# Two more units of a recurrent-attention kernel loaded as 32x32 blocks and turned by VectorE

## The chip, the cores and the metric

The kernel runs on one core of a Trainium2 chip. The metric is the device time of one execution in microseconds. The core has five engines with queues of their own: TensorE (PE; its weight loads are shown apart as PEld), VectorE (DVE), ScalarE (ACT), GpSimd (POOL) and SyncE (SP), which here issues nearly all DMAs.

## What is computed

An attention of the linear, gated kind (float32, B = 4 batches, H = 8 heads, S = 768 steps, D = 48 features) is followed by a feed-forward layer with a maximum over three products:

```python
f = 1.0 / (1.0 + np.exp(-f_logit))
for t in range(S):
    state = f[:, :, t, :, None] * state + np.einsum('bhd,bhe->bhde', k[:, :, t], v[:, :, t])
    y[:, :, t] = np.einsum('bhd,bhde->bhe', q[:, :, t], state)
x = y.transpose(0, 2, 1, 3).reshape(B * S, H * D)          # 3072 x 384
h = np.maximum(np.maximum(x @ w1, x @ w2), x @ w3)         # 384 -> 768
out = h @ w_out                                            # 768 -> 384
```

The weights come as 64-bit floats; the kernel turns them into 32-bit ones itself.

## The kernel before

**Units.** The attention is cut into 24 units (`NU`). A unit is a chunk of 64 time steps (`C`) of two batches with all eight heads: 128 rows of tokens. Even and odd units take the two pairs of batches. Four units make a group (`GRP`); the feed-forward layer works on groups of 512 tokens.

**One unit.** The gate f, the keys k and the queries q are needed with features on the partitions and time along the free dimension. The sigmoid of f (`sigmoids`) gives the gate; a scan along time from behind (`scan`, L329) gives factors r for the keys, and one from the front (`before`, L347) gives `prod` for the queries. `kh` = k turned times r (`after`, L340), `qh` = q turned times `prod` (L351). `pairs` multiplies kh and qh on TensorE (L392) and VectorE applies the causal mask (`at`, L395). `values` multiplies that with v (L411, L407 in the first group), `sums` adds the unit's keys times values to the state (L436 on TensorE, L444 on VectorE), for which the keys are needed once more with tokens on the partitions (`ks`). `finish` (L500) adds the share of the old state and ScalarE copies the result into `xT` (L506).

**Two ways to turn.** Units below `BY_ROWS` are loaded by rows: one DMA of 192 KB for each of f, k and q (L174), with tokens on the partitions and features along the free dimension. TensorE then turns them with four transposes each (`transposed`, L291) into PSUM. ScalarE takes the sigmoid from PSUM into the gate (L308), and VectorE multiplies kh and qh from PSUM. `keys` turns kh back with four TensorE transposes (L367), and ScalarE copies them into `ks` (L369).

Units from `BY_ROWS` on are loaded in pairs as blocks: eight DMAs of 64 or 32 KB for each of f, k and q (L183), which put every 32x32 block of tokens by features at the partitions where its features will lie. ScalarE takes the sigmoid from SBUF (L311), VectorE turns gate, kt and qt with one instruction each (`turned`, L296), and GpSimd multiplies kh and qh. `keys_by_blocks` makes `ks` with 16 instructions of VectorE (L382), four at each of four places of the loop.

Both ways share the same buffers: `room` holds four slots of a unit for each of f, k and q, in two tiles. Unit u by rows uses slot u % 4; a pair by blocks uses tile u // 2 % 2 as a whole.

**The weights.** 24 pieces are loaded into `raw` and `placed` and rounded to float32: ScalarE prepares (L240, L241, L244), VectorE joins the high bits (L254), and GpSimd adds the rest (L258) into `w_in` or, for pieces 18 to 23, into `w_out`. `apart` (L715) subtracts the first weight matrix from the other two. So the maximum becomes a linear part plus a maximum against zero.

**The first group.** `ffn_first` runs along with units 4 to 8. It computes the products of x with the weights (L537, two of the PSUM banks of pool `ps_f`), takes ScalarE's copy (L765) and VectorE's maximum (L767) into `hm`, turns the first weight matrix (`turn`, L737 and L738), forms the linear part's matrix (`linear`, L745, copied by L749), places the weights for the later groups by DMA (`place`, L454 and L461), and computes the outputs (`outputs`, L563). GpSimd's `mix_in` (L805) and `mix` (L587) prepare sums of weights. The later groups run with fewer products, from `placed` and mixed weights (L836, L609).

**Order.** The order is written out by hand, and the instructions of each engine stand in that order. In the loop over units 4 to 23, `fill(part)` puts a budgeted share of the feed-forward work between the steps of the attention. Each engine works through its own queue in order; semaphores tie them together. Which PSUM bank of a pool a new tile gets is settled when the program is built.

Of the kernel before, what the change touches and what calls it, by code (L numbers as in the profile page):

```python
# [55 lines left out]
def kernel(  # L56
# [15 lines left out]
    NU = B // 2 * (S // C)  # L72
# [5 lines left out]
    GRP = 4  # L78
# [11 lines left out]
    def fast():  # L90
        ctx = ExitStack()
        with ctx:
# [55 lines left out]
                    nc.vector.memset(t.rearrange("p (h d) -> p h d", d=DP)[:, :, D:], 0.0)  # L148

            NLD = 4  # L150
            BY_ROWS = 8
            v_tiles = [keep.tile([128, H, DP], FP32, name=f"v_ld{i}") for i in range(NLD)]
            for t in v_tiles:
                nc.gpsimd.memset(t[:, :, D:DP], 0.0)
# [12 lines left out]
            def load(u, queues=one, names="fkq"):  # L167
                for nm, src in (("f", f_logit), ("k", k), ("q", q)):
                    if nm not in names:
                        continue  # L170
                    if u < BY_ROWS:

# [114 lines left out]
            def transposed(nm, u, name="tr"):  # L287

                t = {"tr": ps_tr, "p": ps_f}[name].tile([128, HP, 2, C], FP32, name=name)
                for hp in range(HP):  # L290
                    nc.tensor.transpose(t[:, hp].rearrange("p a t -> p t a"), slots[nm][u % 4][:, hp * 128:(hp + 1) * 128],  # L291
                                        ident)
                return t.rearrange("p h a t -> p a h t")

            def turned(out, x):
                nc.vector.transpose(out.rearrange("p x (n t) -> p x n t", t=32), x.rearrange("p n x d -> p x n d"))  # L296
# [8 lines left out]
            def sigmoids(u):  # L305
                gate = gate_tiles[u % 2]
                if u < BY_ROWS:
                    nc.scalar.activation(by_batch(gate)[:, :, :, 1:], transposed("f", u), AF.Sigmoid)  # L308
# [5 lines left out]
            def features(nm, u):  # L314

                if u < BY_ROWS:
                    return transposed(nm, u, "p" if u < GRP - 1 else "tr")
# [6 lines left out]
            def scan(u):  # L324
                gate = gate_tiles[u % 2]
                if u >= BY_ROWS:
                    turned(gate[:, :, 1:], ready[u])
# [6 lines left out]
            def after(u):  # L334
# [4 lines left out]
                nc.gpsimd.tensor_copy(ends[:, u, :], whole)  # L339
                (nc.vector if u < BY_ROWS else nc.gpsimd).tensor_tensor(  # L340
                    kh.rearrange("p h a t -> p a h t"), kt,
# [3 lines left out]
            def before(u):  # L345
# [4 lines left out]
                qh = by_batch(work.tile([128, 2 * HP, C], FP32, name="qh", bufs=3))  # L350
                (nc.vector if u < BY_ROWS else nc.gpsimd).tensor_tensor(qh, qt, by_batch(prod[:, :, 1:]), op=ALU.mult)  # L351
                ready[u]["qh"] = qh
# [8 lines left out]
            def keys(u):  # L361

                if u < min(BY_ROWS, NU - 2):
                    kh = ready[u]["kh"]
                    tr_s = ps_tr.tile([UT, HP, 128], FP32, name="tr")
                    for hp in range(HP):
                        nc.tensor.transpose(tr_s[:, hp, :], kh[:, hp].rearrange("p a t -> p (a t)"), ident)  # L367
                    ks = work.tile([UT, H, DP], FP32, name="ks")
                    nc.scalar.copy(ks.rearrange("s h d -> s (h d)"), tr_s.rearrange("s a d -> s (a d)"))  # L369
                    ready[u]["ks"] = ks  # L370

            def keys_by_blocks(u, n):

                if BY_ROWS <= u < NU - 2:
                    kh = ready[u]["kh"]
                    if n == 0:
                        ready[u]["ks"] = work.tile([UT, H, DP], FP32, name="ks")
                    ks = ready[u]["ks"].rearrange("s (hp par) d -> s hp par d", par=2)
                    a, t0 = divmod(n * 32, C)
                    for p0 in range(0, 128, 32):  # L380
                        par, e0 = divmod(p0, DP)
                        nc.vector.transpose(ks[n * 32:(n + 1) * 32, :, par, e0:e0 + 32], kh[p0:p0 + 32, :, a, t0:t0 + 32])  # L382
# [131 lines left out]
            def pack(u0, u1, xT, queues=one):  # L514

                t = slice(u0 * UT, (u1 + 1) * UT)
                for par in range(2):
                    p0 = par * DP
                    queues[par].dma_start(out=xT[p0 + D:p0 + DP, 0:NK, t], in_=xT[p0:p0 + D, NK, t])
# [399 lines left out]
            def fill(ns):  # L919
                budget[0] += ns  # L920
                while budget[0] > 0 and pending:
                    try:
                        budget[0] -= next(pending[0])
                    except StopIteration:
                        pending.pop(0)
# [18 lines left out]
            with tc.manual_schedule():  # L944
# [78 lines left out]
                for u in range(GRP, NU):  # L1023
                    n = u + 1
                    part = EARLY if u < 2 * GRP else PART
                    fill(part)
                    keys(u)
                    keys_by_blocks(u, 2)
                    if u > GRP:
                        finish(u - 1, xT)  # L1030
                        if u % GRP == 3:
                            pack(0, 2, xT)
                        elif u % GRP == 0:
                            pack(3, 3, xT)
                    if u % GRP == 0:
                        if u > GRP:
                            packed[u // GRP - 1] = xT
                            pending.append(ffn(u // GRP - 1, xT))
                        xT = x_tiles[u // GRP % 2]
                    pairs(u)  # L1040

                    if u + 2 < BY_ROWS:
                        load(u + 2)
                    if BY_ROWS <= u + 3 < NU and u % 2:
                        load(u + 3, one, "fkq" if u % GRP == 1 else "f")
                    if u + 2 < NU:
                        load_v(u + 2)
                    if n < NU:
                        if n < BY_ROWS:
                            sigmoids(n)  # L1050
                        scan(n)
                    check_range(u - CHECKS, 0)
                    fill(part)
                    keys_by_blocks(u, 3)
                    if n < NU:
                        after(n)
                        before(n)
                    fill(part)
                    if BY_ROWS <= u + 2 < NU and u % GRP == 0:
                        load(u + 2, one, "k")  # L1060
                    values(u)
                    if n < NU:
                        carry(n)
                    check_range(u - CHECKS, 1)
                    fill(part)
                    if BY_ROWS <= u + 2 < NU and u % GRP == 0:
                        load(u + 2, one, "q")
                    keys_by_blocks(n, 0)
                    fill(part - 1000 if u < 2 * GRP else part)
                    keys_by_blocks(n, 1)  # L1070
                    check_range(u - CHECKS, 2)
                    if u + 2 >= CHECKS:
                        check_load(u + 2 - CHECKS)
                    if BY_ROWS <= u + 2 < NU:
                        sigmoids(u + 2)
# [272 lines left out]
```

## Time and profile before

| quantity | before |
|---|---|
| median of 3 runs (lowest to highest) | 423.31 us (423.26 to 423.86) |
| profiled execution: its time, and its span | 423.43 us, 421.7 us |
| busy TensorE, VectorE, ScalarE, GpSimd | 402.8, 264.5, 180.2, 235.2 us |
| mean granted clock of TensorE | 0.996 |
| turns of f, k, q on TensorE (L291): matrix instructions, length of one | 96, 0.27 us |
| turns of keys on TensorE (L367) | 32, 0.27 us |
| turns on VectorE: gate, kt, qt (L296) | 48, 0.66 to 0.72 us |
| turns of keys on VectorE (L382) | 224, 0.30 us |
| mean DMA share from 50 to 63.4, 63.4 to 78.3, 78.3 to 95, 95 to 106 us | 0.93, 0.72, 0.82, 0.25 |

Times in profile rows are microseconds from the span's start unless marked ns. A row of a timeline has start, length, engine, line, operation, output and inputs with their shapes, and a count; in brackets stand the idle time of the engine ahead of it and what ended it. Matrix instructions overlap, so a step of TensorE is best measured from one row's start to the next one's. The profiled execution's time is longer than its span by what lies around it. TensorE transposes one 128x128 float32 tile in an instruction, and a row "x4" is one of f, k, q or the keys of one unit.

### The profile page before, as it was taken

What the parts mean: (1) busy time and instruction counts of PE and PEld (TensorE: products, weight loads), DVE (VectorE), ACT (ScalarE), POOL (GpSimd) and SP (SyncE); (2) the same over time, 40 slices, a digit from 0 to 9 for tenths busy, and PEclk for the clock granted to TensorE, in tenths of its full rate; (3) what the DMA queues carried; (4) which work ended last, traced back from release to release, by engine and by line L of the source; (5) the groups of instructions that cost most, each with busy time, mean ns of one, the idle gap of its engine ahead of it and who ended that gap; (6) DMA issues with size and microseconds to landing.
All of it is one profiled execution on the core that took longest, in us unless ns stands there. A gap on an engine that the chain in (4) does not pass through costs nothing.

```text
span 421.7 us, 11556 instructions
## 1 busy us (share of the span) xinstructions
PE 402.8 (96%) x4650; PEld 338.5 (80%) x4650; DVE 264.5 (63%) x515; ACT 180.2 (43%) x414; POOL 235.2 (56%) x262
## 2 busy tenths in 40 slices
PE   4978899899999999999999999999999999999995
PEld 3756765466668888998889988889988889988994
DVE  6986594843597699868789867889764730002300
ACT  2478676632114442425531444442254524576210
POOL 2189554621988676376586357576556960435600
PEclk9999999999999999999999999999999999999998
DMA  8999897782547654277645276635473010542002
GB/s 169 232 266 284 236 258 112 121 170 67 102 85 129 87 116 66 60 106 101 117 104 95 56 113 87 144 79 89 64 144 91 11 54 9 158 140 75 2 19 60
DMA packets 175129, 47.20 MB, mean 112 GB/s; under 512 B 154016, under 2 KB 172768, under 8 KB 175072
## 3 DMA queue, kind: packets, MB, share of 16 engines
q1 hardware_dynamic: 171600, 45.61, 52.0%
q10 hardware_dynamic: 3472, 0.81, 0.9%
q8 instruction: 37, 0.61, 0.6%
q14 instruction: 20, 0.16, 0.1%
HBM read 37.75 MB, written 4.72 MB: 101 GB/s over the span
## 4 chain that ended last, share of the span: by engine, by line
PE 86%; SPq 5%; DVE 3%; POOL 2%; issue 1%; ACT 1%; DMA 1%; DVEq 0%; POOLq 0%
PE p L836 19%; PE tr L836 16%; PE p L609 15%; PE tr L609 12%; PE p L563 6%; PE p L537 5%; PE p L745 3%; PE y L500 3%; PE y L411 3%; SPq L164 2%; PE a L392 2%; SPq L174 2%; PE y L436 2%; POOL w_in L258 1%; DMA placed<-in_moe_w_dram 1%
## 5 line engine op out<-in xcount | busy, mean ns | idle before, releaser
L836 PE MATMUL tr<-xT,placed 128*128 128x256 f32 x300 | 73.3, 385 | 0.0
L382 DVE STREAM_TRANSPOSE ks<-kh 32x128 f32<-32x128 f32 x224 | 67.7, 302 | 4.6 <-POOL kh L340 1.0
L836 PEld LDWEIGHTS tr<-xT,placed 128*128 128x128 f32 x300 | 55.6, 190 | 9.1 <-ACT hm L844 1.4
L836 PE MATMUL p<-xT,placed 128*128 128x256 f32 x180 | 45.0, 381 | 0.0
L537 PE MATMUL p<-xT,w_in 128*128 128x256 f32 (+1 forms) x108 | 34.4, 459 | 4.9 <-DVE hm L767 2.2
L836 PEld LDWEIGHTS p<-xT,placed 128*128 128x128 f32 x180 | 33.8, 190 | 4.7
L329 DVE TENSOR_TENSOR_SCAN r<-gate,from_one 128x520 f32<-128x520 f32 x24 | 31.3, 1306 | 8.9 <-ACT gate L308 5.9
L617 DVE TENSOR_TENSOR o<-tr,w_in 128x384 f32<-128x384 f32 (+1 forms) x11 | 5.7, 515 | 48.8 <-PE tr L609 43.5
L340 POOL TENSOR_TENSOR kh<-kt,r 128x512 f32<-128x512 f32 x16 | 28.7, 1796 | 10.6 <-DVE kt L296 10.6
L596 POOL TENSOR_TENSOR w_in<-hm 128x256 f32<-128x256 f32 x15 | 10.9, 727 | 40.5 <-DVE hm L887 40.5
L854 POOL TENSOR_TENSOR hm<-hm,rest_bits 128x512 f32<-128x512 f32 x15 | 22.7, 1514 | 19.2 <-ACT hm L844 19.2
L506 ACT COPY xT<-y 64x256 f32<-64x256 f32 (+1 forms) x60 | 22.1, 369 | 24.1 <-PE y L500 23.4
L347 DVE TENSOR_TENSOR_SCAN prod<-gate,from_inv 128x520 f32<-128x520 f32 x24 | 31.9, 1329 | 0.0
L395 DVE TENSOR_TENSOR at<-a,mask 128x512 f32<-128x512 f32 x24 | 16.5, 688 | 24.2 <-PE a L392 23.9
L836 PE MATMUL p<-w_in,placed 128*128 128x256 f32 x120 | 30.0, 379 | 0.0
L537 PEld LDWEIGHTS p<-xT,w_in 128*128 128x128 f32 x108 | 19.3, 190 | 13.0 <-issue 6.2
L258 POOL TENSOR_TENSOR w_in<-top_bits,rest_bits 128x384 uint32<-128x384 uint32 x18 | 21.8, 1218 | 13.5 <-DVE top_bits L254 8.0
L879 DVE TENSOR_TENSOR hm<-tr,hm 128x512 f32<-128x512 f32 x15 | 10.2, 681 | 29.3 <-PE tr L836 19.3
L662 POOL TENSOR_TENSOR o<-top_bits,w_in 128x384 f32<-128x384 f32 x5 | 5.1, 1018 | 41.6 <-ACT w_in L614 41.6
L614 ACT COPY w_in<-p 128x384 f32<-128x384 f32 x15 | 7.2, 480 | 47.3 <-PE p L609 47.3
L280 ACT ACTIVATE raw<-top_bits 128x384 f32<-128x384 f32 x48 | 25.3, 526 | 0.4
L836 PEld LDWEIGHTS p<-w_in,placed 128*128 128x128 f32 x120 | 22.8, 190 | 3.1
(155 smaller groups left out, 888.4 us busy)
## 6 DMA issues: line engine op xcount, KB each, us to landing
raw<-in_moe_w_dram SPq DMA_DIRECT2D x24, 384.0 KB, 4.2
v_ld<-in_v_dram SPq DMA_DIRECT2D x48, 96.0 KB, 3.3
placed<-in_moe_w_dram SPq DMA_DIRECT2D x12, 384.0 KB, 5.7
out_dram<-o SPq DMA_DIRECT2D x46, 96.0 KB, 2.2
placed<-in_moe_w_out_dram SPq DMA_DIRECT2D x6, 384.0 KB, 5.9
raw<-in_moe_w_out_dram SPq DMA_DIRECT2D x6, 384.0 KB, 3.3
f_ld<-in_f_logit_dram SPq DMA_DIRECT2D x32, 64.0 KB, 2.6
k_ld<-in_k_dram SPq DMA_DIRECT2D x32, 64.0 KB, 2.5
```

Of the source, the lines that this page charges most:

```text
L258: nc.gpsimd.tensor_tensor(dst, by(top), by(rest), op=ALU.add)
L280: nc.scalar.activation(over, size, AF.Relu, scale=(-1 / HI_MIN, 1.0)[step - 1], bias=(1.0, -HI_END * (1 - 2.0 ** -24))[step - 1], accum_ou ...
L329: nc.vector.tensor_tensor_scan(r[:, 0:LEN][:, ::-1], flat(gate)[:, ::-1], flat(from_one)[:, ::-1], 1.0, op0=ALU.mult, op1=ALU.max)
L340: (nc.vector if u < BY_ROWS else nc.gpsimd).tensor_tensor(kh.rearrange("p h a t -> p a h t"), kt, by_batch(r[:, 1:LEN + 1].rearrange("p (x ...
L347: nc.vector.tensor_tensor_scan(flat(prod), flat(gate_tiles[u % 2]), flat(from_inv[u % 2]), 1.0, op0=ALU.mult, op1=ALU.max)
L382: nc.vector.transpose(ks[n * 32:(n + 1) * 32, :, par, e0:e0 + 32], kh[p0:p0 + 32, :, a, t0:t0 + 32])
L506: nc.scalar.copy(xT[o, :, t0 + a * C:t0 + (a + 1) * C], y[i, a, 0:HP * C].rearrange("p (h t) -> p h t", h=HP))
L537: nc.tensor.matmul(p if w < TOK else p.rearrange("p (two t) -> p two t", two=2), lhsT=w_in[i][:, kt, j * 128:(j + 1) * 128], rhs=x[:, t.st ...
L563: nc.tensor.matmul(p[:, 0:DM], lhsT=lhsT, rhs=rhs, start=(n == 0), stop=(n == NJ + NK - 1))
L609: nc.tensor.matmul(b[:, p * HD:(p + 1) * HD], lhsT=lhs(p)[:, k], rhs=rhs[:, k], start=id(b) not in begun, stop=(k == HJ - 1), skip_group_c ...
L836: nc.tensor.matmul(b[:, j * HALF:(j + 1) * HALF], lhsT=w[:, (2 * n + j) * 128:(2 * n + j + 1) * 128], rhs=x, start=begin and j == 0, stop= ...
L854: nc.gpsimd.tensor_tensor(out(n, 0), out(n, 0), first, op=ALU.add)
```

## The change

`BY_ROWS` becomes 6: units 6 and 7 are loaded as a pair of blocks and turned by VectorE, their kh and qh are multiplied by GpSimd, and their keys' token rows are made by `keys_by_blocks`. The three other edits adapt the places of the loads: `load(6)` is issued in the iteration of unit 4, where it now loads units 6 and 7 with 24 DMAs; the two later `load` lines leave that pair out; unit 8 is loaded where it was. `sigmoids(6)` and `sigmoids(7)` come at the ends of the iterations of units 4 and 5.

```diff
-            BY_ROWS = 8
+            BY_ROWS = 6
...
-                    if u + 2 < BY_ROWS:
+                    if u + 2 <= BY_ROWS:
                         load(u + 2)
                     if BY_ROWS <= u + 3 < NU and u % 2:
                         load(u + 3, one, "fkq" if u % GRP == 1 else "f")
...
-                    if BY_ROWS <= u + 2 < NU and u % GRP == 0:
+                    if BY_ROWS < u + 2 < NU and u % GRP == 0:
                         load(u + 2, one, "k")
                     values(u)
...
-                    if BY_ROWS <= u + 2 < NU and u % GRP == 0:
+                    if BY_ROWS < u + 2 < NU and u % GRP == 0:
                         load(u + 2, one, "q")
```

## Prediction before the result

> **What bounds the kernel now.** I read the page's busy rows and its chain that ended last, then the chain in order of time, then TensorE's, VectorE's and SyncE's timelines from 50 to 107 us, where units 6 and 7 are prepared.
>
> ```profile
> PE 402.8 (96%) x4650; PEld 338.5 (80%) x4650; DVE 264.5 (63%) x515; ACT 180.2 (43%) x414; POOL 235.2 (56%) x262
> PE 86%; SPq 5%; DVE 3%; POOL 2%; issue 1%; ACT 1%; DMA 1%; DVEq 0%; POOLq 0%
> ```
>
> TensorE sets the end: 86% of the chain is its work, and after 82.25 us its timeline shows no idle time for the next 45 us. An instruction taken off it after 82.25 is worth its length, unless something else becomes late. Before 82.25 it waits three times. TensorE's timeline, the number in brackets being the idle time ahead of the row:
>
> ```profile
> 71.00 0.66 PE L291 MATMUL tr<-ident,f_ld 128*128 128x128 f32 x4
> 71.49 1.02 PE L537 MATMUL p<-xT,w_in 128*128 128x512 f32 x2
> ...
> 72.68 0.60 PE L291 MATMUL tr<-ident,k_ld 128*128 128x128 f32 x4
> 73.12 0.60 PE L291 MATMUL tr<-ident,q_ld 128*128 128x128 f32 x4
> 74.64 2.81 PE L537 MATMUL p<-xT,w_in 128*128 128x512 f32 x6 [0.92 <-DVE hm L767]
> ...
> 82.25 2.82 PE L745 MATMUL p<-w_out,w_in 128*128 128x384 f32 x8 [0.61 <-POOL state L357]
> 84.90 0.60 PE L367 MATMUL tr<-ident,kh 128*128 128x128 f32 x4
> ```
>
> The turns of unit 6 (L291) end in a wait for VectorE. VectorE's timeline for the same stretch:
>
> ```profile
> 71.14 0.69 DVE L395 TENSOR_TENSOR at<-a,mask 128x512 f32<-128x512 f32 x1 [5.01 <-PE a L392]
> 72.46 1.24 DVE L329 TENSOR_TENSOR_SCAN r<-gate,from_one 128x520 f32<-128x520 f32 x1 [0.62 <-ACT gate L308]
> 73.73 0.21 DVE L332 RECIPROCAL from_inv<-r 128x8 f32<-128x8 f32 x1
> 73.86 0.64 DVE L767 SCALAR_TENSOR_TENSOR hm<-hm,p 128x512 f32<-128x512 f32 x1
> ...
> 75.35 1.36 DVE L254 SCALAR_TENSOR_TENSOR top_bits<-placed,top_bits 128x384 uint32<-128x384 uint32 x1
> 76.63 0.68 DVE L340 TENSOR_TENSOR kh<-tr,r 128x512 f32<-128x512 f32 x1
> 77.23 1.72 DVE L347 TENSOR_TENSOR_SCAN prod<-gate,from_inv 128x520 f32<-128x520 f32 x1
> ```
>
> L767, which frees the PSUM bank for TensorE's 74.64 row, stands behind unit 6's scan.
>
> **What the Trainium skill says.** "SBUF — State Buffer", SBUF: two separate sides: VectorE instructions with two SBUF inputs and GpSimd instructions share one port pair, and whoever starts second waits for the whole of the other. The trace agrees: L254 takes 0.55 alone but 1.36 at 75.35, beside GpSimd's L258 of 75.11 to 76.30, and ends 0.4 after it. "VectorE: DVE Perf Modes", The three transpose paths: VectorE turns only 32x32 blocks and writes SBUF. The trace prices that: 0.70, 0.71 and 0.68 for gate, kt and qt of a unit (L296), 0.303 for each of 16 key turns (L382). "DMA: Bandwidth & Descriptors", Measured: transfers under 64 KB are dominated by descriptors (for GpSimd-issued DMAs; these are SyncE's). Here 24 block loads of 64 and 32 KB take the queue 14.8 us (63.42 to 78.23), 0.617 each; an unhindered 192 KB row load takes 0.62.
>
> **The change part by part.**
>
> *TensorE, removed.* By starts of neighbouring rows: f 0.49 and k with q 0.87 to 0.96 for unit 6, f 0.49, k and q 0.87 for unit 7, keys 0.53 for each. Sum some 3.8 us.
>
> *Unit 6's f, k, q: worth nothing.* VectorE now turns gate (0.70) where it waited 0.62 for ScalarE's gate. After unit 8's mask (L395, 101.84) the turn and scan start at 102.44 and 103.18: 1.34 from mask to scan, against 1.32 here. So L767 stays at 73.9, TensorE's next row at 74.65, and 1.4 us becomes idle time. ScalarE's sigmoid, 0.62 against 0.60, now runs from SBUF with an iteration's lead.
>
> *VectorE and GpSimd, added.* For each unit 3 turns (2.09) and 16 key turns (4.85) on VectorE, less two multiplications (0.68 and 0.69), which go to GpSimd (kh about 1.0 to 1.2, qh 1.17). The key turns stand ahead of L767, L254 and L395. Following the order from 76.65, with the port rule:
> - kt to 77.35; the scan waits for L258 (to 77.88), ends 79.0; GpSimd's kh ends 80.05; qt ends 79.75.
> - L254 of piece 20 waits for kh, ends 80.5; L444 to 81.0; four key turns to 82.2; L767 to 82.85 instead of 82.1.
> - GpSimd: qh to 81.65, L258 (piece 20) to 82.65, state to 83.45. L254 (21) waits for it, ends 83.85; L258 (21) 84.95.
> - Four key turns to 85.1; L254 (22 and 23) to 86.15; L258 (22) 87.15, L258 (23) 88.15, against 86.13 before.
>
> *What TensorE sees.* L745 no longer takes the bank that L767 frees but the one that the last turn's copy frees (L738, 82.15): it starts at 82.25 as now. Products cost 0.645 each. The fourth needs piece 21: ready at 84.2, gets it at 85.0. Then L500 and L392 (1.06) to 86.7; the fifth waits for piece 22 to 87.2, the sixth for piece 23 to 88.2. Before, the sixth began at 87.8, so TensorE is 0.4 late there: keys 6 and f 7 (1.02) are eaten. After it k and q 7 (0.87) and keys 7 (0.53) remain: 1.4 - 0.4 = 1.0 us gained. Unit 6's keys must be turned for L436: the last four follow unit 7's scan and end near 91.6, L436 comes near 93.3. Unit 7's first twelve end near 98.5, within VectorE's 6.88 us of idle time before 101.84; the last four follow unit 8's scan, and L436 needs them near 107.
>
> *SyncE's queue.* Out: six row loads, 8.6 us (52.79 to 58.63 and 60.59 to 63.33). In: 24 block loads. The first six meet the same backlog of weights and end about 58.6; 18 x 0.617 = 11.1 brings the last to 69.7. f of both units is issued by 60 and lands 2.9 to 4.8 later, by 65, where ScalarE reaches it; behind that sigmoid stands hm's copy (67.89), whose bank is wanted at 72.4. k lands near 68, q near 73, wanted at 76.6 and 79. Past it move v of unit 6, unit 8's loads, v 7, the DMAs into placed (L454, L461), v 8 and what follows: unit 8 starts at 71.1, 7.7 late, the second placed tile ends at 102.2 instead of 94.8. Its reader, GpSimd's L805, runs to about 105, just when unit 8's kt is turned. SyncE's idle time from 94.8 to 98.9 takes up 4 us; w_lin, the pads of xT and unit 10 come 3 us late or less, with more than that in hand. Cost nothing; bound 0 to 2. If f came after 71.5, all would slip by its lateness.
>
> *ScalarE, removed.* Two key copies of 0.59: off the path.
>
> **The sum.** The profiled execution took 423.43 (span 421.7 and 1.7 around it): 423.43 - 1.0 = 422.4. The median of the runs is 0.12 lower: 422.3. The unseen part is who gets the port when both engines wait. If VectorE never loses it, the pieces are 0.7 to 1.4 earlier; if it always loses, they are nearly 3 later. I take the alternation that 82.72 to 86.13 shows: three L258 in 3.41 with one L254 between.
>
> **Rivals.**
> - *The pieces are in time.* If L258 (23) ends by 87, all 2.4 us removed after 82.25 count: 423.3 - 2.4 = 420.9; small waits: 421.5. For: L254 is 0.55 where it is alone. Against: four key turns now precede it twice.
> - *All given back.* Piece 23 ends 1.0 later than I reckon, at 89.2: about 423.3, no change. For: VectorE has no free moment from 76.6 to 94.7.
> - *VectorE becomes the bound (slower).* GpSimd's work is queued back to back, so it may hold the port: L254 (20) then waits for qh too (1.2), L254 (21) for a further L258 (1.0), the last pair for another 0.7. Piece 23 comes 2.9 later and 1.9 is lost: 425.2. It decides from 89.2 for piece 23 on: each us beyond is a us lost. Against: the one place where both wait shows alternation.
> - *The block loads are late.* Six row DMAs become 24 while the queue is backed up. Decides only if f lands after 71.5: 6 us away; 5% within the slower case.
> - *It doesn't do what it says.* Excluded: in the changed program's order those turns are gone from TensorE and stand on VectorE.
>
> **How the numbers follow.** Forecast 0.45 (around 422.3; two thirds of it gains more than 0.2%, which is 0.85 us and about what a measurement of this kernel can tell from no change), pieces in time 0.22, given back 0.15, slower 0.18. Faster: 0.32 + 0.22 = 0.54; same: 0.13 + 0.15 = 0.28; slower 0.18. From 421.1 to 424.5 leaves out the best of the second case and most of the last, together some 0.19. The cases that gain have their own range, 421.1 to 422.5.
>
> **What would show it.** TensorE's row near 74.6 should wait about 2.3 us for L767 instead of 0.92. L745 should start near 82.3 and wait for GpSimd's L258 ahead of its fourth, fifth and sixth products, 0.3 to 0.8 each. L382 should count 256 instead of 224, L291 32 transposes of f fewer by 8 (likewise k and q), L411 of unit 6 start near 92.7. L805's first row should start near 103. Wrong: TensorE waiting for L382 at L436, for ScalarE before 75, or L745 starting after 83.

## The result, and the profile after

| | before | after |
|---|---|---|
| median (lowest to highest), 20 runs each | 423.31 us (422.97 to 425.35) | 422.64 us (421.88 to 423.35) |
| ratio, 95% interval | | 0.998 (0.9972 to 0.9988) |
| profiled execution: time, span | 423.43, 421.7 | 423.19, 421.5 |

The change is worth 0.67 us, where 1.0 was forecast. A second set of 22 runs (experiment 5) gave 422.73 and a ratio of 0.9986 (0.9978 to 0.9994). So the size is near; in the profile of after the way to it is not the one forecast. The page of after, busy rows and the group of the key turns:

```profile
PE 401.8 (95%) x4618; PEld 336.0 (80%) x4618; DVE 275.0 (65%) x549; ACT 178.8 (42%) x412; POOL 241.9 (57%) x266
...
PE 87%; SPq 3%; DMA 3%; DVE 3%; ACT 1%; issue 1%; POOL 1%; DVEq 0%; ACTq 0%; POOLq 0%
...
L382 DVE STREAM_TRANSPOSE ks<-kh 32x128 f32<-32x128 f32 x256 | 77.4, 302 | 5.1 <-POOL kh L340 1.0
```

The turns moved as announced: 256 key turns on VectorE where there were 224, 32 matrix instructions fewer, and TensorE still sets the end. But TensorE's busy time fell by 1.0 us only (the second profile of after, experiment 5 below, has 400.1, which is 2.7 less than before). TensorE's timeline says why. Three rows of before, then the rows of after:

```profile
69.41 0.60 PE L367 MATMUL tr<-ident,kh 128*128 128x128 f32 x4
...
93.12 0.69 PE L411 MATMUL y<-at,v_ld 64*64 64x64 f32 x32
...
414.43 2.11 PE L609 MATMUL tr<-w_out,w_in 128*128 128x192 f32 x12
```

```profile
69.71 0.60 PE L367 MATMUL tr<-ident,kh 128*128 128x128 f32 x4
...
72.27 0.49 PE L737 MATMUL p<-ident,w_in 128*128 128x128 f32 x3
74.98 4.51 PE L537 MATMUL p<-xT,w_in 128*128 128x512 f32 x6 [2.22 <-DVE hm L767]
79.42 0.69 PE L411 MATMUL y<-at,v_ld 64*64 64x64 f32 x32
...
84.33 2.82 PE L745 MATMUL p<-w_out,w_in 128*128 128x384 f32 x8 [0.66 <-ACT w_in L738]
87.07 0.66 PE L500 MATMUL y<-qh,state 48*48 48x64 f32 x32
...
93.52 0.69 PE L411 MATMUL y<-at,v_ld 64*64 64x64 f32 x32
```

The wait for L767 grew from 0.92 to 2.22 us, and the row behind it starts at 74.98, as foreseen (it is 0.34 later than in before, of which 0.30 is there already at L367). What was not foreseen: the same six instructions take 4.51 us where they took 2.81. L745 starts at 84.33, 2.08 late, and from there to unit 6's L411 TensorE needs 9.19 us where before it needed 10.87. The table by stretches (length, then for each engine busy time and count, then TensorE's granted clock, DMA share and GB/s) gives the reason. The profile's clock record holds only the moments at which the granted clock changed: here full from 10.22 us, half from 75.07, full again from 78.48, half from 419.82. Between changes there lie whole multiples of 3.413 us (19, 1 and 100 here), in every profile of this study. So the table is cut into steps of 3.413 us, counted off from the changes:

```profile
71.66:75.07 3.41, 1.19 (x6) 0.51 (x5) 3.34 (x6) 3.31 (x9) 0.00 (x0) 1.00 0.80 118
75.07:78.48 3.41, 3.41 (x5) 1.35 (x6) 3.41 (x5) 0.41 (x2) 2.47 (x3) 0.50 0.67 84
```

In the first step TensorE was busy for 1.19 of 3.41 us (35%); in the next one it was granted half its clock. Half of 3.41 is 1.71 us, which is the lengthening of the L537 row (4.51 - 2.81 = 1.70). From here on this is called the fall.

**A ruler.** The first 69 us vary from execution to execution: in the profiles of this study TensorE's row L367 of unit 5 starts between 69.0 and 70.5, and the same spread stands at L367 of unit 4 already (53.1 to 54.8), ahead of all that an edit moves on TensorE. So runs are compared by the time since that row's start ("by the ruler"), and no start noise is in them. L745 is the start of the linear part's products, L411 of unit 6 that of its values, L836 that of the next group's products; the last group starts right before the end (in 7, 10 and 11 the earlier pieces themselves hold that row back by 0.4 us against L367 of unit 4, 16.1 us behind it for 15.7 in the others; for those three 0.4 is to be added):

| from L367 of unit 5, us | wait ahead of L537 | to L745 | to L411 of unit 6 | to L836 | to the last group (L609) |
|---|---|---|---|---|---|
| before | 0.92 | 12.84 | 23.71 | 57.49 | 345.02 |
| after, first profile | 2.22 | 14.62 | 23.81 | 57.15 | 344.65 |
| after, second profile (experiment 5) | 2.22 | 12.91 | 23.24 | 56.58 | 344.11 |
| 1: after, gap filled | 0.95 | 12.92 | 23.25 | 56.59 | 344.12 |
| 2: before, with a gap | 2.26 | 14.17 | 25.04 | 58.82 | 346.34 |
| 3: after, L767 first | 0.62 | 11.31 | 23.75 | 57.09 | 344.61 |
| 4: after, keys on TensorE | 2.22 | 14.53 | 24.13 | 57.91 | 345.42 |
| 7: after, L767 first, pieces early | 0.61 | 11.31 | 20.48 | 53.82 | 341.36 |
| 8: before, longer hold | 2.09 | 15.67 | 26.54 | 60.32 | 347.84 |
| 10: after, pieces early | 1.46 | 12.15 | 21.32 | 54.66 | 342.19 |
| 11: before, L767 first, pieces early | none | 11.68 | 22.55 | 56.33 | 343.83 |
| 12: unit 7 alone | 0.92 | 12.84 | 22.44 | 55.78 | 344.53 |

### The profile page after: what moved, and what is told of

The parts are those of the page before. It is cut to its first block, busy times and chain, and to the rows that moved or that the text cites. A ratio compares the mean times of both kernels' runs of the same rounds, so it can differ in the third digit from the quotient of the medians.

```text
span 421.5 us, 11552 instructions
## 1 busy us (share of the span) xinstructions
PE 401.8 (95%) x4618; PEld 336.0 (80%) x4618; DVE 275.0 (65%) x549; ACT 178.8 (42%) x412; POOL 241.9 (57%) x266
## 4 chain that ended last, share of the span: by engine, by line
PE 87%; SPq 3%; DMA 3%; DVE 3%; ACT 1%; issue 1%; POOL 1%; DVEq 0%; ACTq 0%; POOLq 0%
PE p L836 19%; PE tr L836 16%; PE p L609 15%; PE tr L609 12%; PE p L537 6%; PE p L563 6%; PE y L411 3%; PE p L745 3%; PE y L500 3%; PE a L392 2%; PE y L436 2%; SPq L174 2%; DMA raw<-in_moe_w_dram 2%; DMA placed<-in_moe_w_dram 1%; SPq L164 1%
## 5 line engine op out<-in xcount | busy, mean ns | idle before, releaser
L382 DVE STREAM_TRANSPOSE ks<-kh 32x128 f32<-32x128 f32 x256 | 77.4, 302 | 5.1 <-POOL kh L340 1.0
L836 PE MATMUL tr<-xT,placed 128*128 128x256 f32 x300 | 73.4, 385 | 0.0
L836 PEld LDWEIGHTS tr<-xT,placed 128*128 128x128 f32 x300 | 55.6, 190 | 9.1 <-ACT hm L844 1.4
L836 PE MATMUL p<-xT,placed 128*128 128x256 f32 x180 | 45.0, 381 | 0.0
L537 PE MATMUL p<-xT,w_in 128*128 128x256 f32 (+1 forms) x108 | 36.2, 477 | 6.2 <-DVE hm L767 3.5
L340 POOL TENSOR_TENSOR kh<-kt,r 128x512 f32<-128x512 f32 x18 | 31.2, 1732 | 11.4 <-DVE kt L296 11.4
L836 PEld LDWEIGHTS p<-xT,placed 128*128 128x128 f32 x180 | 33.8, 190 | 4.7
L537 PEld LDWEIGHTS p<-xT,w_in 128*128 128x128 f32 x108 | 19.9, 195 | 15.4 <-issue 8.6
L836 PE MATMUL p<-w_in,placed 128*128 128x256 f32 x120 | 30.0, 379 | 0.0
L258 POOL TENSOR_TENSOR w_in<-top_bits,rest_bits 128x384 uint32<-128x384 uint32 x18 | 22.1, 1233 | 13.1 <-DVE top_bits L254 8.1
L836 PEld LDWEIGHTS p<-w_in,placed 128*128 128x128 f32 x120 | 22.8, 190 | 3.1
```

The source lines that it names most:

```text
L258: nc.gpsimd.tensor_tensor(dst, by(top), by(rest), op=ALU.add)
L340: (nc.vector if u < BY_ROWS else nc.gpsimd).tensor_tensor(kh.rearrange("p h a t -> p a h t"), kt, by_batch(r[:, 1:LEN + 1].rearrange("p (x ...
L537: nc.tensor.matmul(p if w < TOK else p.rearrange("p (two t) -> p two t", two=2), lhsT=w_in[i][:, kt, j * 128:(j + 1) * 128], rhs=x[:, t.st ...
L836: nc.tensor.matmul(b[:, j * HALF:(j + 1) * HALF], lhsT=w[:, (2 * n + j) * 128:(2 * n + j + 1) * 128], rhs=x, start=begin and j == 0, stop= ...
```

## The experiments

Three theories were put to the test. Theory A: taking unit 6's turns from TensorE leaves a standstill that costs TensorE its clock. Theory B: those six products were slow for something that ran beside them. Theory C: the pieces of w_out (the last six weight pieces, which L745 multiplies) would have taken the gain in any case. The numbers of the experiments are labels; they are told in the order of the argument. Each one's "before" ran beside it, so its ratio counts more than its median.

**1. The gap filled.** In after:

```diff
+            def idle_turns(count):
+                t = ps_tr.tile([128, HP, 128], FP32, name="tr")
+                for i in range(count):
+                    nc.tensor.transpose(t[:, i % HP], ident, ident)
...
                         if n < BY_ROWS:
                             sigmoids(n)
+                        if n == 6 and 4:
+                            idle_turns(4)
...
+                    if n == 6 and 8:
+                        idle_turns(8)
                     if n < NU:
                         after(n)
```

> The kernel after, with twelve TensorE transposes of the identity matrix added where unit 6's turns of f, k and q stood (four behind the gates' sigmoid, eight ahead of the output product of the unit before); nobody reads what they write, so they add TensorE work and nothing else. Theory A (TensorE's granted clock falls because TensorE stands still for 2.2 us ahead of L767's product): the standstill shrinks to about 1 us, the clock stays at 1.00 from 75 to 80 us, the six products of L537 behind it take 2.8 us again instead of 4.5, TensorE is 1.7 us earlier at L411 of unit 5 and at L745, and then two or three of L745's products wait 0.2 to 0.5 us for pieces of w_out, so about 1.2 us off the end against the profile of after: about 421.5. Theory B (those products are slow from something that runs beside them): L537 stays at 4.5, and the time is that of after or a little more. Theory C (the pieces of w_out are next in line anyway): L537 at 2.8, but L745's products end where they did, and the time is within 0.4 us of after.

Measured: 422.72 us, ratio 0.9977 (0.9968 to 0.9986). TensorE's timeline (L937 is the idle turn):

```profile
73.25 1.04 PE L937 MATMUL tr<-ident 128*128 128x128 f32 x8
75.25 2.81 PE L537 MATMUL p<-xT,w_in 128*128 128x512 f32 x6 [0.95 <-DVE hm L767]
...
82.90 2.17 PE L745 MATMUL p<-w_out,w_in 128*128 128x384 f32 x6 [0.66 <-ACT w_in L738]
85.50 0.91 PE L745 MATMUL p<-w_out,w_in 128*128 128x384 f32 x2 [0.43 <-POOL w_out L258]
```

With useless work in the gap the six products take 2.81 again. One profile would not settle that, since after itself has executions without the fall (experiment 5). The mean clock of all executions, a rough measure of the fall (see experiment 5), does: one of 21 here is at 0.995 or less, against 22 of 42 in after. The same VectorE turns and loads ran beside the products, so B falls. L745 comes 1.70 earlier than in the first profile of after, but 0.53 is all that is left at the end: its fourth product waits for a piece. The median is 0.78 below the before beside it, where after's two sets have 0.67 and 0.52, so a gain over after is not clear of noise. A is right on the cause, C on what comes behind it.

**2. The gap in the kernel before.** In before, behind unit 6's scan:

```diff
                         scan(n)
+                        if n == 6:
+                            for _ in range(2):
+                                nc.vector.transpose(o_four.rearrange("t g c -> t (g c)")[:, 0:512],
+                                                    flat(from_one)[:, 0:512])
```

> The kernel before, with two VectorE transposes of 128x512 added between unit 6's scan and L767; they read a tile that is there already and write a scratch tile that nobody reads. They hold L767 back by about 1.4 us, so TensorE stands still for 2.3 us ahead of its product, as in the kernel after, with all of unit 6's turns still on TensorE. Theory A: the granted clock falls to about half behind the gap, the six products of L537 take about 4.5 us, TensorE is 1.4 + 1.7 = 3.1 us late at L745, and some of that is left at the end: 424.8 to 426.4. Theory B: the clock stays at 1.00, L537 at 2.8, and the end is later by 1.4 us at most: 423.3 to 424.7.

Measured: 425.45 us, ratio 1.0058 (1.004 to 1.0076), the four executions 424.41, 424.72, 426.18 and 426.68. The profiled one is the shortest, and its clock did not fall although the gap was 2.26 us:

```profile
71.35:74.76 3.41, 1.97 (x13) 1.26 (x11) 2.72 (x5) 3.32 (x8) 0.00 (x0) 1.00 0.79 97
74.76:78.17 3.41, 2.59 (x6) 1.06 (x6) 3.41 (x7) 0.50 (x2) 1.57 (x2) 1.00 0.76 98
```

A as it stood would not have this. Steps counted off from the clock record explain it: here a boundary (74.76) fell into the gap (73.32 to 75.58) and shared it out, 58% and 76% busy. Two groups of executions, 1.9 us apart, fit that, but four are few, and their mean clocks (0.996 twice in the short ones, 0.996 and 0.995 in the long ones) do not tell the groups apart.

**5. After, once more.** No edit; the refined theory A' (the fall depends on where the step boundaries lie) was put to the test.

> The kernel after, unchanged, once more. The clock records of the first profiles come in steps of 3.413 us; in after the step from 71.66 to 75.07 held nearly the whole standstill (TensorE 35% busy) and the next step ran at half clock, while in the kernel before with a gap of 2.26 us a step boundary fell into the gap (steps 58% and 76% busy) and no clock was lost. Theory A': the clock falls in some executions only, as the step boundaries happen to lie. Then a profile of after shows either the fall (L537's six products 4.5 us) or none (2.8 us, L745 1.7 us earlier and then 0.2 to 0.7 us of waits for pieces of w_out, the stretch from L367 of unit 5 to L836 about 0.5 us shorter than in the first profile); runs with a mean clock of 0.995 or less take 0.4 to 0.6 us longer than those at 0.997 or more; the median is 422.3 to 422.9. Rival: the fall is there in every execution, and the times don't part by the mean clock.

Measured: 422.73 us, ratio 0.9986 (0.9978 to 0.9994). This profile has no fall. TensorE's timeline and the table of the same steps:

```profile
74.59 2.81 PE L537 MATMUL p<-xT,w_in 128*128 128x512 f32 x6 [2.22 <-DVE hm L767]
...
82.24 2.17 PE L745 MATMUL p<-w_out,w_in 128*128 128x384 f32 x6 [0.66 <-ACT w_in L738]
84.84 0.91 PE L745 MATMUL p<-w_out,w_in 128*128 128x384 f32 x2 [0.43 <-POOL w_out L258]
85.69 0.66 PE L500 MATMUL y<-qh,state 48*48 48x64 f32 x32
...
86.91 5.73 PE L745 MATMUL p<-w_out,w_in 128*128 128x384 f32 x16
92.57 0.69 PE L411 MATMUL y<-at,v_ld 64*64 64x64 f32 x32
```

```profile
70.64:74.05 3.41, 1.73 (x29) 0.90 (x21) 2.92 (x5) 3.30 (x8) 0.00 (x0) 1.00 0.76 111
74.05:77.46 3.41, 2.87 (x14) 1.19 (x17) 3.41 (x6) 1.07 (x4) 1.84 (x2) 1.00 0.73 93
```

The same program with the same gap of 2.22 us: the boundary at 74.05 cuts it, 51% and 84% busy, and the six products take 2.81. The 42 executions of both sets of after part as expected: the 22 with a mean clock of 0.995 or less have a median of 422.83, the 17 at 0.997 or more one of 422.22, 0.61 apart. (The mean also holds the last steps of the program, so it sorts roughly.) The median of after is thus a mixture.

The two profiles of after also show why the fall costs so little. It makes L745 1.71 late, but from L745 to unit 6's L411 the one without a fall needs 10.33 us and the one with it 9.19: 1.14 us of waits and refills for pieces, which a late L745 does not have. Left at the end: 0.57 by the ruler (56.58 against 57.15).

**8. A longer hold in before.** As experiment 2, with `range(4)`.

> The kernel before with four of the added VectorE transposes ahead of L767 instead of two, which nobody reads: TensorE stands still for about 3.6 us, longer than one step of 3.413 us. Theory A': wherever the boundaries lie, one step has TensorE busy for less than half of it, so the next one runs at half clock in every execution: the profile shows it, L537 takes 4.5 us for six, and the time is 2.8 + 1.7 us over before: 427 to 428.5. Rival (no link between the gap and the clock): clock at 1.00, L537 at 2.8, 426.3 or less.

Measured: 426.66 us, ratio 1.0067 (1.0049 to 1.0085). The gap was not 3.6 but 2.09 us: in this program the bank for L537 is one that ScalarE's copy L738 frees, not L767, so the four turns did not hold TensorE as reckoned, and the time is below what was expected. But this profile has what experiment 2's lacks:

```profile
73.83:77.25 3.42, 1.33 (x6) 0.64 (x5) 3.28 (x7) 2.24 (x6) 0.00 (x0) 1.00 0.78 95
77.25:80.66 3.41, 3.41 (x7) 0.88 (x6) 3.41 (x6) 0.00 (x0) 1.73 (x2) 0.50 0.69 131
```

The kernel before, with all its turns on TensorE and a gap shorter than experiment 2's, loses its clock when one step holds the gap (39% busy). By the ruler it ends 2.82 late: L537 comes 1.17 later and takes 1.67 longer (4.48). So blocks are not needed for the fall; that VectorE's turns are not enough for it, experiments 1, 2 and 5 show, which have such turns and no fall. It belongs to the standstill and its place in the step. A fall in every execution, as expected for a gap longer than a step, was not tried with a gap of 2.09; one of the four executions (425.35, mean clock 0.998) looks like one without it.

**4. The keys back on TensorE.** In after, units 6 and 7 keep their blocks, but `keys` turns them (the condition in `keys` and in `keys_by_blocks` gets 8 for `BY_ROWS`).

```diff
-            BY_ROWS = 6
+            BY_ROWS, KEYS_BY_ROWS = 6, 8
...
-                if u < min(BY_ROWS, NU - 2):
+                if u < min(KEYS_BY_ROWS, NU - 2):
...
-                if BY_ROWS <= u < NU - 2:
+                if KEYS_BY_ROWS <= u < NU - 2:
```

> The kernel after, with one part of the change undone: units 6 and 7 get f, k and q as blocks as in after, but their keys' token rows are again turned by TensorE, 0.53 us of TensorE for each unit, and VectorE loses 64 turns of 0.302 us. By my step 5 the keys of unit 7 are worth 0.53 us on the path and those of unit 6 lie where TensorE has 0.5 us to spare, so 0.4 to 1.1 us slower than after, 423.1 to 423.8. The rival, that VectorE's key turns hold back the pieces of w_out and so L745: as fast as after or up to 0.5 us faster, with the pieces of L258 ending 1 to 2 us earlier. Under theory A the gap and the clock's fall stay as in after, since the keys stand behind both.

Measured: 423.53 us, ratio 0.9997 (0.9986 to 1.0008). Its profile has the fall, as the first of after: by the ruler 0.77 later at the end, 0.41 of it between L745 and L411 of unit 6 and 0.44 behind, less 0.09. So the keys are worth about 0.4 us each. The nine executions with a mean clock of 0.995 or less have a median of 423.99, the ten at 0.997 or more 422.71, now 1.28 apart where after has 0.61. That fits pieces that, without VectorE's key turns, are in time in an execution without the fall, so that nothing covers the fall any more; there is no profile of such an execution, so this is not shown.

**3. L767 ahead of unit 6's scan.** In after:

```diff
-            ROUNDED = (5, 7, 8, 10, 10, 11, 11, 12, 12, 13, 14, 15, 16, 17, 18, 20, 21, 22)
+            behind_hm, ROUNDED = [], (5, 7, 8, 10, 10, 11, 11, 12, 12, 13, 14, 15, 16, 17, 18, 20, 21, 22)
...
                             nc.vector.scalar_tensor_tensor(hm[:, j, t], hm[:, j, t], 0.0, p, op0=ALU.max, op1=ALU.max)
+                            [scan(behind_hm.pop()) for _ in behind_hm[:]]
...
-                        scan(n)
+                        behind_hm.append(n) if n == 6 else scan(n)
```

> The kernel after, with L767 (the second multiplication of the gates' feed-forward) issued ahead of unit 6's scan on VectorE instead of behind it; the scan follows it at once. Theory A: TensorE's standstill ahead of that product is about 0.5 us, the clock stays at 1.00, L537 at 2.8 us, TensorE is 3 to 3.6 us earlier than in after at L411 of unit 5 (about 76 us) and at L745; then the pieces of w_out set the third to sixth products of L745, which wait some 1.3 to 2.3 us in all, so 1.2 to 1.7 us off the end: about 421.2. Theory B: L537 stays near 4.5, TensorE is earlier by the 1.7 us of the shorter gap alone, and the end by 1 us or less. If the pieces take everything back, the time is within 0.4 us of after.

Measured: 423.11 us, ratio 1.0001 (0.9984 to 1.0019). The 421.2 expected did not come, and no gain over before is clear of noise (by the ruler 0.41 is left, by the median 0.39), although L745 starts 1.60 earlier by the ruler than in the second profile of after.

```profile
80.95 1.53 PE L745 MATMUL p<-w_out,w_in 128*128 128x384 f32 x4 [0.66 <-POOL kh L340]
83.32 0.91 PE L745 MATMUL p<-w_out,w_in 128*128 128x384 f32 x2 [0.84 <-POOL w_out L258]
85.66 0.91 PE L745 MATMUL p<-w_out,w_in 128*128 128x384 f32 x2 [1.42 <-POOL w_out L258]
```

A product is two instructions here: the third and fourth product wait 0.84 and 1.42 us for pieces. The scan, 1.1 us later by the ruler, pushes VectorE's kt and all behind it by 0.5, and the last piece ends at 18.98 by the ruler against 18.47. The pieces are the wall. The three executions with a mean clock of 0.995 or less are the slowest (424.68, 425.38 and 427.18), and they raise the ratio. An estimate from the rows above: a step that held both waits, 2.26 us, would be 34% busy, so these waits can make a fall of their own; no profile of such an execution was taken.

**10. The pieces two places earlier.** In after, one line:

```diff
-            ROUNDED = (5, 7, 8, 10, 10, 11, 11, 12, 12, 13, 14, 15, 16, 17, 18, 20, 21, 22)
+            ROUNDED = (5, 7, 8, 10, 10, 11, 11, 12, 12, 13, 14, 15, 16, 19, 20, 21, 22, 24)
```

> The kernel after with the last pieces of w_out rounded two places earlier, and L767 where it was (behind unit 6's scan). The gap of 2.2 us and the clock's fall in some executions stay. Where the clock does not fall, the second profile of after had 1.1 us of waits and refills for pieces between L745 and L411 of unit 6; these should go: 420.9 to 421.4. Where it falls, nothing covers the 1.7 us any more: 422.4 to 423.1, about as before this edit. So the executions part into two groups 1.5 us apart by their mean clock, where those of after are 0.6 us apart. Rival: the pieces were not what took the gain, and all executions stay where those of after are.

Measured: 420.44 us, ratio 0.9933 (0.9918 to 0.9949).

```profile
73.78 2.81 PE L537 MATMUL p<-xT,w_in 128*128 128x512 f32 x6 [1.46 <-ACT w_in L738]
...
81.43 2.82 PE L745 MATMUL p<-w_out,w_in 128*128 128x384 f32 x8 [0.66 <-ACT w_in L738]
84.18 0.67 PE L500 MATMUL y<-qh,state 48*48 48x64 f32 x32
```

All the waits for pieces are gone: L745 to L411 takes 9.17 us, as in the first profile of after, 1.16 less than in the second. A further 0.76 was not expected: with this order L537 gets a bank that L738 frees, and the gap shrinks to 1.46 us. By an estimate such a gap leaves a step at least 57% busy wherever the boundary lies (1 - 1.46/3.41). The five executions lie within 420.26 to 421.12 with mean clocks of 0.997 and 1.0, so the two groups that were expected did not appear.

**7. Both edits of 3 and 10 in after.**

> L767 ahead of unit 6's scan as in the run before, and with it the last pieces of w_out rounded two places earlier (the last five entries of ROUNDED are 19, 20, 21, 22, 24 for 17, 18, 20, 21, 22), in the 5 us in which VectorE stood idle ahead of unit 5's L395. If the pieces were what took that run's 3.6 us back: L745 starts near 81 us and its eight products wait 0.3 us at most for pieces, L411 of unit 6 starts near 90.5 us, and 420.3 to 421.2 comes out, the fastest of all. Rival: unit 6's qh, state and keys on POOL and VectorE are next in line, or the earlier ACT work holds the gates' copies back; then 422 to 423.

Measured: 419.89 us, ratio 0.992 (0.9906 to 0.9935), the fastest of all and 0.4 under the range expected.

```profile
69.25 0.60 PE L367 MATMUL tr<-ident,kh 128*128 128x128 f32 x4
...
72.91 2.81 PE L537 MATMUL p<-xT,w_in 128*128 128x512 f32 x6 [0.61 <-DVE hm L767]
...
80.56 2.82 PE L745 MATMUL p<-w_out,w_in 128*128 128x384 f32 x8 [0.66 <-ACT w_in L738]
83.31 0.66 PE L500 MATMUL y<-qh,state 48*48 48x64 f32 x32
...
89.73 0.69 PE L411 MATMUL y<-at,v_ld 64*64 64x64 f32 x32
...
410.61 2.11 PE L609 MATMUL tr<-w_out,w_in 128*128 128x192 f32 x12
```

No product of L745 waits for a piece, though it starts at 80.56. By the ruler 3.66 us are saved at the end, 3.3 with the 0.4 ahead of it.

**11. The same two edits in before.**

> The kernel before with both edits of the fastest run so far: L767 ahead of unit 6's scan, and the last pieces two places earlier; units 6 and 7 in rows, turned by TensorE. If the fastest run needs the change: only TensorE's 0.9 us of waiting for L767 goes here, TensorE then has no pause from 73 us on, 422.2 to 422.8; the change is worth 2.3 to 2.9 us on top of it (TensorE loses 2.7 us of turns and 1.0 us of keys, less a gap of 0.6). Rival: those two edits bring the gain themselves and the change little: 421 or less.

Measured: 422.69 us, ratio 0.9988 (0.9978 to 0.9997).

```profile
69.58 0.60 PE L367 MATMUL tr<-ident,kh 128*128 128x128 f32 x4
...
73.72 2.74 PE L537 MATMUL p<-xT,w_in 128*128 128x512 f32 x6
...
81.26 2.82 PE L745 MATMUL p<-w_out,w_in 128*128 128x384 f32 x8 [0.61 <-DVE hm L767]
...
413.41 2.11 PE L609 MATMUL tr<-w_out,w_in 128*128 128x192 f32 x12
```

The edits alone bring 1.19 us by the ruler, 0.8 with the 0.4 ahead of it: the wait for L767 ahead of L537 is gone. On top of them the change is worth 2.47 by the ruler (343.83 - 341.36), and in the medians, each against the runs of before beside it, 2.74 (3.36 - 0.62).

**6, 9 and 12. Unit 7 alone.** With `BY_ROWS` at 7, unit 6 by rows and unit 7 as blocks.

```diff
-            BY_ROWS = 6
+            BY_ROWS = 7
...
-                    elif u % 2 == 0:
+                    if u % 2 == 0 and u + 1 >= BY_ROWS:
```

> The change for unit 7 alone: unit 6 comes in rows and is turned by TensorE, keys too, as in before; unit 7 comes as blocks as in after. By my steps 1 to 3 unit 6's share of the change is worth nothing or less, so this should have all of the gain without the gap: TensorE waits 0.9 us for L767 as in before, the clock stays at 1.00, f, k and q of unit 7 leave 1.36 us of the stretch from L745 to L411 of unit 6 and its keys 0.44 us behind it, and the pieces of w_out end at 86 us as in before since no key turns of unit 6 stand among them: 421.6 to 422.3, no run with a clock fall at 75 us. Rival: unit 6's share carries gain of its own (0.53 us of its keys), so this is slower than after, 422.7 to 423.1.

Measured: 428.77 us. In this kernel unit 7's blocks overwrite unit 6's rows, since both lie in one tile, so unit 6's part of the output is not computed from its data, and TensorE stood 5.59 us waiting for q of unit 6 behind that load. Of unit 7 alone it tells nothing. In the next one unit 6's rows went into slot 0 (`rows[nm][0 if u == 6 else u % 4]`, and so for `slots`).

> The change for unit 7 alone again, now with unit 6's rows in the slots that unit 4 has left (in the run before, unit 6's rows and unit 7's blocks lay in one tile). Unit 6 is turned by TensorE, keys too. Theory: unit 6's f, k and q are worth nothing and make the gap. TensorE waits 0.9 us for L767, the clock stays at 1.00; between L745 and L411 of unit 6 TensorE has 1.36 us less to do than in before and behind it 0.5 us less (keys of unit 7); the pieces of w_out end at 86 us as in before. From L367 of unit 5 to the last group, 345.02 us in before: 343.2 to 343.8; time 421.5 to 422.2, no execution with a clock fall at 75 us. Rival: without unit 6's share the same pieces bind, and less than 0.5 us is left: 422.8 to 423.3.

Measured: 435.3 us; it tells nothing either, for the reason that the next expectation gives: TensorE waited 6.5, 1.1 and 3.4 us for f, k and q. The last one moves unit 8's loads:

```diff
-                    if BY_ROWS <= u + 3 < NU and u % 2:
+                    if BY_ROWS <= u + 3 < NU and u % 2 and u != 5:
...
                         before(n)
+                    if u == 5:
+                        load(8, one, "fkq")
```

> The change for unit 7 alone, with unit 8's block loads issued behind unit 6's last turn: in the run before, they were issued ahead of it and overwrote the slots in which unit 6's rows lay, so its TensorE waited for them and its time says nothing. Unit 6 comes in rows (in unit 4's slots) and is turned by TensorE, keys too; unit 7 comes as blocks; unit 8's loads start near 73.5 us instead of 71.4. Theory: unit 6's f, k and q are worth nothing and make the gap. TensorE waits 0.9 us for L767 as in before, the clock stays at 1.00 in every execution, 1.36 us leave the stretch from L745 to L411 of unit 6 and 0.5 us behind it, and no key turns of unit 6 stand among the pieces. From L367 of unit 5 to the last group (345.02 us in before, 344.11 in the second profile of after): 343.2 to 343.8, and 421.5 to 422.2. Rival: the pieces bind here too, or unit 8's later loads cost something, and it comes out between after and before, 422.7 to 423.4.

Measured: 423.27 us against 423.87 of before beside it, ratio 0.999 (0.9976 to 1.0005). Up to L836 the profile is as the theory has it: the wait for L767 is 0.92, no fall, L745 starts at 12.84 by the ruler as in before, L411 of unit 6 is 1.27 earlier and L836 1.71, where the second profile of after has 0.91. So without unit 6's share the change brings more up to here. Then 1.22 us is given back. TensorE's and GpSimd's timelines:

```profile
125.21 1.03 PE L836 MATMUL p<-xT,placed 128*128 128x256 f32 x4
...
129.71 1.13 PE L836 MATMUL p<-xT,placed 128*128 128x256 f32 x4 [0.49 <-POOL xT L820]
```

```profile
105.70 2.07 POOL L805 TENSOR_TENSOR placed<-placed 128x768 f32<-128x768 f32 x1 [11.30 <-DMA placed<-w_in]
107.71 0.19 POOL L339 COPY ends<-r 128x8 f32<-128x8 f32 x1
...
128.12 1.53 POOL L820 TENSOR_TENSOR xT<-xT 128x256 f32<-128x256 f32 x2
```

SyncE's queue ends the second placed tile at 104.93 us, 2.3 later than in the second profile of after. Some 2.0 of that is not the moved loads but three row loads for unit 6, 0.65 to 0.68 each from start to start, that this edit adds: the pair's blocks are still loaded whole. L805 starts at 105.70, and GpSimd then works without a break until L820, for which TensorE waits 0.49. The rest of the 1.22 is lost by 158 us, with GpSimd still about 1 us later than in after; that it has the same cause is argued, not shown. In after the same row stood like this (second profile):

```profile
103.07 1.97 POOL L805 TENSOR_TENSOR placed<-placed 128x768 f32<-128x768 f32 x1 [6.86 <-DMA placed<-w_in]
104.99 0.19 POOL L339 COPY ends<-r 128x8 f32<-128x8 f32 x1
105.88 1.98 POOL L340 TENSOR_TENSOR kh<-kt,r 128x512 f32<-128x512 f32 x1 [0.71 <-DVE kt L296]
```

The 0.71 us of idle time there was all the margin that after's later loads had left. The expected 343.2 to 343.8 is missed. The rival named late loads; here they are in the main loads that the experiment itself added, so what unit 7 alone would be worth at the end stays open.

## Why the prediction was right or wrong

- **Unit 6's f, k and q are worth nothing.** Right where the clock does not fall: in the second profile L745 starts at 12.91 by the ruler, in before at 12.84, and with unit 6 left on TensorE (12) at 12.84. The wait for L767 was put at about 2.3 and is 2.22. The step that failed is that this idle time costs nothing. Where one step of the clock holds most of it, TensorE runs at half clock for the next 3.41 us: 1.71 at L745, 0.57 at the end.
- **The order with the port rule.** Right to 0.3 us. By the second profile, moved by the 0.08 that its ruler starts earlier: L254 of piece 20 ends at 80.5 (80.5 forecast), L767 at 82.9 (82.85), L258 of piece 21 at 84.9 (84.95), the last at 87.9 (88.15).
- **What TensorE sees.** Right in kind, two terms mis-sized against each other: the products lose 1.14 us on pieces where the three waits were put at 1.65 in all, and the turns between L745 and L411 are worth 1.68 (10.87 - 9.19) where they were put at 1.89 (0.53 + 0.49 + 0.87). L411 of unit 6 is 0.47 earlier than before, as forecast (1.0 less the 0.53 of keys 7); keys 7 bring 0.44. Together 0.91 for 1.0. Part of this closeness is luck: the forecast read 87.8 for the start of the sixth product in before, where its own row gives 87.64 (86.99 and one product of 0.645), and with that its working gives 0.84; the pieces then came 0.27 earlier than reckoned.
- **SyncE's queue.** Unit 8's loads at 71.36 in the first profile (71.1 forecast), the second placed tile's end at 102.34 (102.2), L805 at 103.48 (about 103): right, and it cost nothing (from L836 to the last group all three profiles need 287.5). But the margin behind L805 was the 0.71 us of idle time shown in experiment 12, thin beside a bound of 0 to 2.
- **The sum.** 1.0 forecast, 0.91 without a fall, 0.34 to L836 with one; the median of the mixture is 0.67 below before. The median of 422.3 is met by the executions at a mean clock of 0.997 or more (422.22).
- **The rivals.** Pieces in time came true in after only where the clock fall made L745 late, and cost more than it gave; with the pieces really early the change is worth 2.47 us (7 against 11), near the 2.4 of that rival, though 0.37 of it lies ahead of L745 (11.68 and 11.31), where that rival counted nothing. VectorE as the bound did not come: the port alternated as taken. "L745 starting after 83" was named as a sign of error; it was one, of a cause that no rival had.

## What to carry to other kernels

Before work is taken off an engine whose next step waits for another engine, ask whether the time becomes anything but a longer wait, and whether the wait becomes long enough to change the clock; a profile's clock record in its own steps shows it, a mean does not. When a change takes work off the bound and little comes back, look for the next producer in line: here five numbers of a schedule, which moved work into an idle stretch of VectorE, turned a gain of 0.7 us into 2.9. Of the 1.92 that this brought by the ruler against the second profile, 1.16 is the pieces; the other 0.76 is a change of bank that nobody had planned. Compare profiles from a row that no edit touches, and take a second profile before a cause is settled: one and the same program showed both pictures.

## What of the hardware was not expected

The Trainium skill, "TensorE: Matmul & The Clock Gate", What's actually happening, says that the clock halves after at least one idle window of about 3.4 us, and that the windows of 3413 ns run freely. The second part agrees with these records: steps of 3.413 us, at another phase in each profile. On the first the measurement decides: a standstill of 2.1 to 2.2 us was enough. Steps with TensorE 35% (after), 40% (experiment 4) and 39% busy (experiment 8) were followed by one at half clock; steps with 49% (a later one, 81.7 to 85.1, of experiment 3), 51, 57 and 58% were not.

All fourteen profiles agree when they are cut into such steps from the first entry of the clock record on. Of 1677 steps at full clock, 20 were followed by one at half clock. All 20 were at most 40% busy; most stand at the end of the program, the highest in experiment 2, whose fall at 75 us did not come:

```profile
416.10:419.51 3.41, 1.37 (x9) 1.07 (x7) 0.72 (x2) 0.00 (x0) 0.00 (x0) 1.00 0.36 82
419.51:422.59 3.08, 0.00 (x0) 0.00 (x0) 0.00 (x0) 0.00 (x0) 0.00 (x0) 0.50 0.18 50
```

The other 1657 were at least 49% busy. Where between 40 and 49% the bound lies, and whether it is a matter of busy time or of something that goes with it, stays open. An estimate from these numbers: for 40% a step must hold 2.05 us of a gap, for 49% 1.75 us. With the boundary anywhere in the 3.41 us with the same chance, a gap of 2.22 us then takes the clock in 45 to 62% of the executions; 22 of after's 42 (52%) had a mean clock of 0.995 or less.
